# Recurrent-memory attention with a GeGLU block: TensorE work of the recurrent stage moved to column groups of 32, and one output written before another

## The chip, the cores and the metric

The kernel runs on one core of a Trainium2 chip. The metric is the device time of one execution in microseconds. The engines are TensorE (PE; its weight loads are listed as PEld), VectorE (DVE), ScalarE (ACT), GpSimd (POOL) and SyncE (SP). The kernel uses POOL and SP mostly to issue DMAs.

## The reference

All inputs are bf16. Two branches share the input `x` (2048 rows of 1024), and a gate for each row mixes them.

```python
def _A_ref(x, mem0, Wq, Wk, Wv, Wo, seg_len):       # 32 heads of 128, M = 8, seg_len = 32
    mask = (idx[:, None] < M) | (idx[:, None] >= idx[None, :])
    mem = mem0
    for s in range(n_seg):                          # 64 segments
        xs = x[:, s * seg_len:(s + 1) * seg_len, :]
        h = jnp.concatenate([mem, xs], axis=1)      # 40 rows
        q, k, v = (einsum('btd,dhe->bhte', h, W) for W in (Wq, Wk, Wv))
        scores = einsum('bhqe,bhke->bhqk', q, k) * scale
        p = softmax(where(mask, scores, -1e9))
        o = einsum('bhte,hed->btd', einsum('bhqk,bhke->bhqe', p, v), Wo)
        mem = o[:, :M, :]
        outs.append(o[:, M:, :])
    return concatenate(outs)

def _B_ref(x, w_gate, w_up, w_down):                # inner size 3584
    return gelu(x @ w_gate) * (x @ w_up) @ w_down

g = sigmoid((x * gate_w).sum(-1, keepdims=True))
out = g * _A_ref(...) + (1 - g) * _B_ref(...)
```

The eight memory rows that a segment gives are the first rows of the next one, so the 64 segments run one after the other.

## The kernel before

**Stages.** The first 600 us or so compute the GeGLU branch with matmuls that use all 128 columns of the array (lines 449 and 494) and transposes of `x` (line 336). Then come the 64 segments, which are called the recurrent stage here.

**A segment's rows.** The 40 rows are split: 24 rows of the segment and the 8 memory rows make `hT` (32 columns), and the 8 first rows of the segment ("ext" rows) do not depend on the memory, so they are computed for four segments at once (`xe`, 32 columns), one or two of the six projections in a segment, ahead of time. Their results go through DRAM (`qk_scr`, `v_scr`) and come back through `qkst` and `vt`.

**Weight streams.** With only 32 rows in a segment, the rows are the stationary operand, and the weights move past them. The four matmuls of one step use the same 32 stationary columns on the four column groups of the array, each with another 512 weight columns, and write 32 partitions each. They are called P (line 955: the projections q, k, v in two halves of 16 heads, eight steps each), E (line 849: the same for the ext rows), O (line 1109: the output projection, 32 steps of 256 columns) and OE (line 1090: the output projection of four segments' ext rows). Part of the weights stays in SBUF and PSUM; the rest is streamed anew in each segment from DRAM into `ring` (line 615, issued on SP). The ring has ten slots, a transfer fills two of them, and each is issued when PE is through with its slots.

**Attention.** Between the streams stand short blocks:
- T (line 993): four 128 x 128 transposes of the projection in `rows`, after which DVE or ACT copies them to `qk`. The ext rows have the same at line 880.
- S (line 1027): eight matmuls of 40 stationary and 40 moving columns, in pairs, one at output partition 0 and one at 64. DVE and ACT then do the softmax (lines 1034 to 1047) and write `pn`.
- P^T (line 1057): four transposes of `pn`, each of 80 stationary columns. DVE copies them to `ptb` (line 1062).
- P V (line 1068): four matmuls with 128 stationary columns of `vt` and 80 moving ones. ACT copies the result to `oT` and `oe`.

Each occurs four times in a segment (heads by eight). At the segment's end ACT copies the first memory result to `rows` (line 1338), two transposes (line 1354) turn it, and DVE writes it into `hT`.

**Output.** DVE multiplies by the gate and adds the other branch's rows: `bo` (line 1364), which four DMAs write out (line 1371). In every fourth segment (`s % 4 == 3`, the "o" segments) the ext rows of four segments are finished as well: DVE writes them into the first 256 columns of `pn` (line 1375), and four more DMAs write those out (line 1382). Both sets are issued on POOL, in the last segment on SP and ACT. `pn` is the buffer that the softmax of the next segment writes.

**Order.** The order of work on each engine is written out by hand, and a small scheduler (`_Sched`) turns reads and writes into semaphore waits. A DMA that reads a buffer holds back the buffer's next writer.

Of the kernel before, what the change touches and what calls it, by code (L numbers as in the profile page):

```python
# [128 lines left out]
def bass_gated_mix__memory_aug_recurrent_mem_tr__geglu_ffn__prompt_kernel(  # L129
# [21 lines left out]
    SEG = 32  # L151
# [16 lines left out]
    with ExitStack() as es:  # L168
# [639 lines left out]
        for s in range(NSEG):  # L808
# [52 lines left out]
            def end_ext(m, h, j):  # L861
                if s == 0:
                    rx, kx, sx = stage(m, h)
                else:
                    flush()
                    rx, kx, sx = rowsx[:, :], RX, "rowsx"
                op("act", lambda e: e.activation(rx, PB[B_X][:, :], ACTF.Copy), r=[P(B_X)], w=kx)  # L867
                if m == "v":
                    def put():
                        op("pool", lambda e: e.dma_start(v_scr[j, h, :, :, :, :].rearrange("g u r c -> (g u r) c"), rx),  # L870
                           r=kx, w=[("vscr", j, h)], dsem="%sv" % sx)
                    vput.append(put) if s == 0 else put()
                    return
                mi = "qk".index(m)

                def go(bank=B_T):
                    def mk(e):
                        ins = None
                        for i in range(4):
                            ins = e.transpose(PBV[bank][:, i * 128:(i + 1) * 128], rx[:, i * 128:(i + 1) * 128], ident[:, :])  # L880
                        return ins
                    op("pe", mk, r=[*kx, ("ident",)], w=[P(bank)])
                    return bank

                def put(bank):
                    st = rx.rearrange("p (u g r i) -> p u g r i", u=GR, g=4, r=EXT)
                    src = PBV[bank][:, 0:512].rearrange("p (i g u r) -> p u g r i", i=4, g=4, u=GR)

                    def cp(e):
                        ins = None  # L890
                        for u in range(GR):
                            ins = e.tensor_copy(st[:, u], src[:, u])  # L892
                        return ins
                    op("dve", cp, r=[P(bank)], w=kx)
                    op("pool", lambda e: e.dma_start(  # L895
                        qk_scr[j * GR:(j + 1) * GR, h, :, mi, :].rearrange("u p x -> p u x"),
                        rx.rearrange("p (u x) -> p u x", u=GR)),
                       r=kx, w=[("qkscr", j, h, mi)], dsem=sx)
                post.append((go, put))
# [89 lines left out]
            def emit_T(m, eng="dve"):  # L989
                def mk(e):  # L990
                    ins = None
                    for i in range(4):
                        ins = e.transpose(PBV[B_T][:, i * 128:(i + 1) * 128], rows[:, i * 128:(i + 1) * 128], ident[:, :])  # L993
                    return ins
                op("pe", mk, r=[("rows",), ("ident",)], w=[P(B_T)])
                src = PBV[B_T][:, 0:512].rearrange("p (i g c) -> p g c i", i=4, g=4)
                if eng == "act":
                    op("act", lambda e: e.activation(qk[:, m, :, 0:SEG, :], src, ACTF.Copy), r=[P(B_T)], w=[("qk", m)])
                else:
                    op("dve", lambda e: e.tensor_copy(qk[:, m, :, 0:SEG, :], src), r=[P(B_T)], w=[("qk", m)])  # L1000
# [19 lines left out]
            def emit_S(o, s=s):  # L1020
                def mk(e):
                    ins = None
                    for i in range(4):
                        for side in range(2):
                            p0 = SIDES[side]
                            gq = 2 * (o % 2) + side
                            ins = e.matmul(PB[B_S][p0:p0 + L, i * L:(i + 1) * L],
                                           lhsT=qk[:, 0, gq, :, i], rhs=qk[:, 1, gq, :, i], start=True, stop=True,
                                           skip_group_check=True)
                    return ins  # L1030
                op("pe", mk, r=[("qk", 0), ("qk", 1), ("qke",)], w=[P(B_S)])
                sv = PB[B_S][0:104, 0:4 * L].rearrange("p (i c) -> p i c", i=4)
# [20 lines left out]
            def emit_PT(o, s=s):  # L1053
                def mk(e):
                    ins = None
                    for i in range(4):
                        ins = e.transpose(PBV[B_PT][0:KEYS, i * 128:i * 128 + 104], pn[0:104, i, :], ident[0:104, 0:104])  # L1057
                    return ins
                op("pe", mk, r=[("pn", 0), ("pn", 2 * SEG), ("ident",)], w=[P(B_PT)])
                src = PBV[B_PT][0:KEYS, 0:512].rearrange("p (i two c) -> p i two c", i=4, two=2)[:, :, :, 0:L]  # L1060
                first = [("z", t) for t in range(NT)] + [("th", t) for t in range(NT)] if s == 0 and o == 0 else []
                op("dve", lambda e: e.tensor_copy(ptb[0:KEYS, :, :, :], src), r=[P(B_PT)], w=[("ptb",)] + first)  # L1062

            def emit_PV(o, s=s):
                def mk(e):
                    ins = None
                    for i in range(4):
                        ins = e.matmul(PB[B_PV][:, i * 80:(i + 1) * 80], lhsT=vt[0:KEYS, o % 2, i * 128:(i + 1) * 128],  # L1068
                                       rhs=ptb[0:KEYS, i, :, :].rearrange("p two c -> p (two c)"), start=True, stop=True)
                    return ins  # L1070
                op("pe", mk, r=[("vt", o % 2), ("vte", o % 2), ("vte", o % 2, 0), ("ptb",)], w=[P(B_PV)])
                src = PB[B_PV][:, 0:320].rearrange("p (i two c) -> p i two c", i=4, two=2)
                dst = oT[:, o % 2, :, :].rearrange("p (two i) c -> p i two c", two=2)
                u = s % GR
                dste = oe[:, o * 8:(o + 1) * 8, u * EXT:(u + 1) * EXT].rearrange("p (two i) c -> p i two c", two=2)
                op("act", lambda e: e.activation(dst, src[:, :, :, 0:SEG], ACTF.Copy), r=[P(B_PV)], w=[("oT", o % 2)])  # L1076
                op("act", lambda e: e.activation(dste, src[:, :, :, SEG:L], ACTF.Copy), r=[P(B_PV)], w=[("oe", o)])
                if o < 2 and s > 0:
                    load_vte(s, 1, o)
# [43 lines left out]
            def begin_o():  # L1123
# [4 lines left out]
                if "o" in jobs:  # L1128
                    for q in range(4):
                        op("pool", lambda e, q=q, j=jobs["o"]: e.dma_start(  # L1130
                            rowsx[32 * q:32 * q + 32, 0:256], b_scr[j * GR:(j + 1) * GR, q, NR:SEG, :]),
                           r=[("bscr", jobs["o"], y) for y in range(GR)], w=[("rowsx", q)], dsem="be%d" % q)

            if s == 0:
                emit_P("q", 0, (0,))
# [214 lines left out]
            if s + 1 < NSEG:  # L1350
                def mk_mem(e):
                    ins = None
                    for x in range(2):
                        ins = e.transpose(PBV[B_PT][:, x * 128:(x + 1) * 128], rows[:, x * 128:(x + 1) * 128], ident[:, :])
                    return ins
                op("pe", mk_mem, r=[("rows",), ("ident",)], w=[P(B_PT)])
                msrc = PBV[B_PT][:, 0:256].rearrange("p (c q r) -> p q c r", c=2, q=4)[:, :, :, NR:SEG]
# [3 lines left out]
                back(1)  # L1361
            if s == 0:
                flush()
            op("dve", lambda e, s=s, B_O=B_O: e.scalar_tensor_tensor(  # L1364
                out=bo[:, :], in0=PB[B_O][:, 0:256], scalar=gseg[:, s:s + 1], in1=bo[:, :], op0=ALU.mult, op1=ALU.add),
               r=[P(B_O)] + [("gseg", "%s%d" % (k, q)) for k in "ab" for q in range(4)], w=[("bo", x) for x in range(4)])
            for put, bank in ends:
                put(bank)
            last = s == NSEG - 1
            for x, (d, b) in enumerate(rows_of(s)):  # L1370
                op(("sp", "act")[x % 2] if last else "pool", lambda e, d=d, b=b: e.dma_start(d, b),  # L1371
                   r=[("bo", x)], w=[("out", s, x)], dsem="%s%d" % ("end" if last else "out", x))
            if "o" in jobs:
                j = jobs["o"]
                op("dve", lambda e, j=j: e.scalar_tensor_tensor(
                    out=pnz[:, 0:256], in0=PB[B_X][:, 0:256], scalar=ge[:, j:j + 1], in1=rowsx[:, 0:256],
                    op0=ALU.mult, op1=ALU.add),
                   r=[P(B_X)] + [("gseg", "e%d%d" % (q, u)) for q in range(4) for u in range(GR)] + RX,
                   w=[("pn", 0), ("pn", 2 * SEG)])
                for q in range(4):  # L1380
                    op(("sp", "act")[q % 2] if last else "pool",
                       lambda e, q=q, j=j: e.dma_start(first_rows(of, j, q), pnz[32 * q:32 * q + 32, 0:256]),
                       r=[("pn", 0)] + [("out", x, q) for x in range(max(0, j * GR - 1), j * GR + GR - 1)],
                       w=[("oute", j, q)], dsem="%s%d" % ("ende" if last else "oute", q))
            if s > GR and s % GR == 2 and s // GR + 2 < NG:
                load_xe(s // GR + 2)

# [40 lines left out]
```

## Time and profile before

| what | value |
|---|---|
| time, median of 3 runs | 2500.43 us (2494.03 to 2503.6) |
| profiled execution | 2493.11 us, its span in the profile 2491.2 us |
| mean granted TensorE clock | 0.993 |
| DMA packets | 293698, 780.59 MB, mean 313 GB/s |
| weight stream into `ring` | 1153 DMAs of 512 KB and 63 of 256 KB, median 6.2 and 5.9 us from issue to landing |
| T, line 993 | 1024 transposes, median 219 ns for one |
| S, line 1027 | 2048 matmuls, median 198 ns |
| P^T, line 1057 | 1024 transposes, median 209 ns |
| P V, line 1068 | 1024 matmuls, median 202 ns |

Matmuls are pipelined: the duration of one reaches from its start to its modelled end, and the next may start long before that. So what a matmul costs PE is read from start to start. The idle time in a timeline's brackets is that before an instruction on its engine, with what ended it. "issue" is time in which the engine waited for nothing that the profile shows.

### The profile page before, as it was taken

The numbers are of one execution on the slowest core, as the hardware profiler recorded it, in microseconds if no ns is written. First come the engines' busy times: TensorE is split into PE (matmuls) and PEld (weight loads), VectorE is DVE, ScalarE is ACT, GpSimd is POOL, SyncE is SP. The second block draws the span as 40 slices with busy tenths as digits, with TensorE's granted clock in tenths as the row PEclk, the third lists the DMA queues.
The fourth block names the chain that finished last, engine by engine and source line by source line (L and its number), as shares of the span: only waits on it lengthen the run. The fifth ranks groups of instructions, "written<-read, shape, count | busy, mean of one in ns | idle before, by whom it ended". The sixth has DMA issues, their size and how long they took to land.

```text
span 2491.2 us, 77615 instructions
## 1 busy us (share of the span) xinstructions
PE 2242.6 (90%) x33993; PEld 1110.2 (45%) x33993; DVE 1209.9 (49%) x3499; ACT 933.0 (37%) x2196; POOL 653.8 (26%) x1162
## 2 busy tenths in 40 slices
PE   9999999999889898888889888988898888888887
PEld 4444444444444444444444444444444444444443
DVE  5626264451445455445454545445454445454544
ACT  4314132220434344434344434434343444343433
POOL 1010103102332323232323323332323232323222
PEclk9999999999999999999999999999999999999999
DMA  8727354468999999999999999999999999999997
GB/s 270 260 71 255 97 179 123 144 231 287 320 335 368 351 363 366 358 348 360 351 365 360 365 345 365 359 359 353 346 362 349 366 349 359 345 371 359 365 367 291
DMA packets 293698, 780.59 MB, mean 313 GB/s; under 512 B 48840, under 2 KB 112568, under 8 KB 292592
## 3 DMA queue, kind: packets, MB, share of 16 engines
q1 hardware_dynamic: 249344, 720.25, 79.6%
q0 software_dynamic: 43872, 55.31, 7.1%
q8 instruction: 268, 4.39, 0.7%
q14 instruction: 70, 0.57, 0.1%
q10 hardware_dynamic: 144, 0.06, 0.0%
HBM read 748.00 MB, written 37.22 MB: 315 GB/s over the span
## 4 chain that ended last, share of the span: by engine, by line
PE 57%; DMA 26%; DVE 10%; issue 3%; ACT 2%; POOL 2%; DVEq 0%; POOLq 0%; ACTq 0%
DMA ring<-w_scr 21%; PE pbb L955 7%; PE pba L955 7%; PE pbc L849 4%; PE pbb L1109 3%; DMA out_dram<-pn 3%; PE pbe L1057 2%; PE pba L1109 2%; PE pba L449 2%; PE pbb L449 2%; PE pbc L449 2%; PE pbh L449 2%; PE pbe L449 2%; PE pbg L449 2%; PE pbf L449 2%
## 5 line engine op out<-in xcount | busy, mean ns | idle before, releaser
L955 PE MATMUL pba<-arena,hT 128*32 128x512 bf16 x4416 | 360.4, 383 | 0.4 <-issue 0.4
L955 PE MATMUL pbb<-arena,hT 128*32 128x512 bf16 x4416 | 354.7, 383 | 0.0
L721 POOL DMA_DIRECT2D vt<-v_scr x252 | 147.7, 588 | 429.3 <-PE pbe L1068 234.6
L1000 DVE COPY qk<-pbe 128x512 bf16<-128x512 bf16 x129 | 89.3, 692 | 260.0 <-PE pbe L993 253.7
L849 PE MATMUL pbc<-arena,xe 128*32 128x512 bf16 x2208 | 215.0, 383 | 0.7 <-ACT rowsx L867 0.5
L1040 ACT ACTIVATE pbd<-pbd 104x160 f32<-104x160 f32 x256 | 72.3, 283 | 381.6 <-DVE pbd L1038 381.6
L1062 DVE COPY ptb<-pbe 80x320 bf16<-80x320 bf16 x256 | 82.1, 321 | 273.5 <-PE pbe L1057 273.5
L1371 POOL DMA_DIRECT2D out_dram<-bo x252 | 125.9, 507 | 224.4 <-DVE bo L1364 222.5
L955 PE MATMUL pba<-ring,hT 128*32 128x512 bf16 x1478 | 152.5, 385 | 29.0 <-DMA ring<-w_scr 26.4
L955 PE MATMUL pbb<-ring,hT 128*32 128x512 bf16 x1474 | 150.8, 384 | 16.2 <-DMA ring<-w_scr 15.5
L961 ACT ACTIVATE rows<-pba 128x512 bf16<-128x512 f32 x128 | 76.6, 598 | 214.0 <-PE pba L955 213.9
L1047 DVE TENSOR_TENSOR pn<-pbd,rr 104x256 bf16<-104x256 f32 (+1 forms) x512 | 142.4, 319 | 28.3 <-DMA out_dram<-pn 20.0
L955 PEld LDWEIGHTS pba<-arena,hT 128*32 128x32 bf16 x4416 | 110.5, 96 | 92.6 <-issue 3.4
L955 PEld LDWEIGHTS pbb<-arena,hT 128*32 128x32 bf16 x4416 | 106.8, 96 | 90.7 <-issue 2.4
L895 POOL DMA_DIRECT2D qk_scr<-rowsx x60 | 47.5, 791 | 356.6 <-DVE rowsx L892 309.6
L961 ACT ACTIVATE rows<-pbb 128x512 bf16<-128x512 f32 x128 | 76.6, 598 | 169.5 <-PE pbb L955 169.1
L1057 PE MATMUL pbe<-ident,pn 104*80 104x104 bf16 x1024 | 95.6, 216 | 39.8 <-DVE pn L1047 29.6
L1109 PE MATMUL pba<-ring,oT 128*32 128x256 bf16 x1792 | 104.1, 279 | 25.9 <-DMA ring<-w_scr 18.7
L1041 DVE TENSOR_REDUCE rs<-pbd 104x4 f32<-104x160 f32 x256 | 83.2, 325 | 89.4 <-ACT pbd L1040 89.4
L1109 PE MATMUL pbb<-ring,oT 128*32 128x256 bf16 x1792 | 113.6, 277 | 13.8 <-DMA ring<-w_scr 9.1
L1076 ACT ACTIVATE oT<-pbe 128x256 bf16<-128x256 f32 x256 | 97.2, 380 | 76.4 <-PE pbe L1068 76.4
L1109 PE MATMUL pba<-arena,oT 128*32 128x256 bf16 x2176 | 112.4, 279 | 11.6 <-ACT oT L1076 10.6
(266 smaller groups left out, 4454.3 us busy)
## 6 DMA issues: line engine op xcount, KB each, us to landing
ring<-w_scr SPq DMA_DIRECT2D x1153, 512.0 KB, 6.2
arena<-in_B_w_gate_dram SPq DMA_DIRECT2D x27, 1024.0 KB, 5.4
arena<-in_B_w_up_dram SPq DMA_DIRECT2D x27, 1024.0 KB, 7.9
ring<-w_scr SPq DMA_DIRECT2D x63, 256.0 KB, 5.9
qkst<-qk_scr POOLq DMA_DIRECT2D x126, 64.0 KB, 5.4
qk_scr<-rowsx POOLq DMA_DIRECT2D x60, 128.0 KB, 5.1
arena<-in_B_w_down_dram SPq DMA_DIRECT2D x7, 1024.0 KB, 11.7
arena<-in_A_Wk_dram SPq DMA_DIRECT2D x6, 1024.0 KB, 6.6
```

The source lines that it names most:

```text
L449: ins = e.matmul(PB[bank][:, :], lhsT=wv[:, kc, col:col + 128], rhs=xb[:, kc, :], start=(kc == 0), stop=(kc == KC - 1))
L721: op("pool", lambda e: e.dma_start(vt[2 * SEG:KEYS, par, :], v_scr[s // GR, h, 2 * par:2 * par + 2, s % GR, :, :]), r=[("vscr", s // GR, h ...
L849: ins = e.matmul(PB[B_X][32 * gq:32 * gq + 32, :], lhsT=xe[:, us[-1], :], rhs=us[gq // 2][0][gq % 2], start=(n == 0), stop=(n == KC - 1), ...
L955: ins = e.matmul(PB[bank][32 * gq:32 * gq + 32, :], lhsT=hT[:, kc, :], rhs=us[gq // 2][0][gq % 2], start=(x == 0), stop=(x == KC - 1), ski ...
L961: op("act", lambda e: e.activation(rows[:, :], PB[bank][:, :], ACTF.Copy), r=[P(bank)], w=[("rows",)])
L1000: op("dve", lambda e: e.tensor_copy(qk[:, m, :, 0:SEG, :], src), r=[P(B_T)], w=[("qk", m)])
L1041: op("dve", lambda e: e.tensor_reduce(rsv, sv, AX.X, ALU.add), r=[P(B_S)], w=[("rs",)])
L1047: op("dve", lambda e, c0=c0, k0=k0, n=n: e.tensor_tensor(out=pn[0:104, :, c0:c0 + 2 * n].rearrange("p i (two c) -> p i two c", two=2), in0 ...
L1057: ins = e.transpose(PBV[B_PT][0:KEYS, i * 128:i * 128 + 104], pn[0:104, i, :], ident[0:104, 0:104])
L1076: op("act", lambda e: e.activation(dst, src[:, :, :, 0:SEG], ACTF.Copy), r=[P(B_PV)], w=[("oT", o % 2)])
L1109: ins = e.matmul(PB[B_O][32 * q:32 * q + 32, 0:256], lhsT=oT[:, o % 2, k, :], rhs=u[q // 2][:, (q % 2) * 256:(q % 2 + 1) * 256], start=(o ...
L1371: op(("sp", "act")[x % 2] if last else "pool", lambda e, d=d, b=b: e.dma_start(d, b), r=[("bo", x)], w=[("out", s, x)], dsem="%s%d" % ("en ...
```

## The change

Every transpose and matmul of the recurrent stage that used 128, 80 or 40 stationary columns is split so that each part uses at most 32 columns, and writes the partitions of one column group, as the weight streams do: T and the transposes of lines 880 and 1354 become four for one, S two for one (32 and 8 of its 40 columns), P^T three for one (32, 32 and 16), P V four for one. The results and their places are the same.

In the "o" segments the ext rows are now finished and sent out before the segment's own rows, by the new `out_first`: DVE's line 1375 goes ahead of line 1364, and the four DMAs of line 1382 ahead of the four of line 1371. In the last segment the order stays as it was.

```diff
@@ transposes of the ext rows (line 880)
-  ins = e.transpose(PBV[bank][:, i * 128:(i + 1) * 128], rx[:, i * 128:(i + 1) * 128], ident[:, :])
+  for y in range(0, 128, 32):
+      ins = e.transpose(PBV[bank][y:y + 32, i * 128:(i + 1) * 128],
+                        rx[:, i * 128 + y:i * 128 + y + 32], ident[:, :])
@@ emit_T (line 993), and likewise the memory's transposes (line 1354)
-  ins = e.transpose(PBV[B_T][:, i * 128:(i + 1) * 128], rows[:, i * 128:(i + 1) * 128], ident[:, :])
+  for j in range(0, 128, 32):
+      ins = e.transpose(PBV[B_T][j:j + 32, i * 128:(i + 1) * 128],
+                        rows[:, i * 128 + j:i * 128 + j + 32], ident[:, :])
@@ emit_S (line 1027)
-  ins = e.matmul(PB[B_S][p0:p0 + L, i * L:(i + 1) * L],
-                 lhsT=qk[:, 0, gq, :, i], rhs=qk[:, 1, gq, :, i], start=True, stop=True, ...
+  for c0, c1 in ((0, SEG), (SEG, L)):
+      ins = e.matmul(PB[B_S][SIDES[side] + c0:SIDES[side] + c1, i * L:(i + 1) * L],
+                     lhsT=qk[:, 0, gq, c0:c1, i], rhs=qk[:, 1, gq, :, i], start=True, stop=True, ...
@@ emit_PT (line 1057)
-  ins = e.transpose(PBV[B_PT][0:KEYS, i * 128:i * 128 + 104], pn[0:104, i, :], ident[0:104, 0:104])
+  for j in range(0, KEYS, 32):
+      n = min(32, KEYS - j)
+      ins = e.transpose(PBV[B_PT][j:j + n, i * 128:i * 128 + 104], pn[0:104, i, j:j + n], ident[0:104, 0:104])
@@ emit_PV (line 1068)
-  ins = e.matmul(PB[B_PV][:, i * 80:(i + 1) * 80], lhsT=vt[0:KEYS, o % 2, i * 128:(i + 1) * 128],
-                 rhs=ptb[0:KEYS, i, :, :].rearrange("p two c -> p (two c)"), start=True, stop=True)
+  for j in range(0, 128, 32):
+      ins = e.matmul(PB[B_PV][j:j + 32, i * 80:(i + 1) * 80],
+                     lhsT=vt[0:KEYS, o % 2, i * 128 + j:i * 128 + j + 32],
+                     rhs=ptb[0:KEYS, i, :, :].rearrange("p two c -> p (two c)"), start=True, stop=True,
+                     skip_group_check=True)
@@ end of a segment (from line 1361 on)
+  last = s == NSEG - 1
+  if not last:
+      out_first()              # lines 1375 and 1382
   op("dve", ... out=bo ...)    # line 1364
   for put, bank in ends:
       put(bank)
-  last = s == NSEG - 1
   for x, (d, b) in enumerate(rows_of(s)):
       op(... dma_start(d, b) ...)   # line 1371
-  if "o" in jobs:
-      ...                      # lines 1375 and 1382
+  if last:
+      out_first()
```

## The prediction

> **What bounds the kernel now.** I read the page first: engine shares and the chain that ended last.
>
> ```profile
> span 2491.2 us, 77615 instructions
> PE 2242.6 (90%) x33993; PEld 1110.2 (45%) x33993; DVE 1209.9 (49%) x3499; ACT 933.0 (37%) x2196; POOL 653.8 (26%) x1162
> PE 57%; DMA 26%; DVE 10%; issue 3%; ACT 2%; POOL 2%; DVEq 0%; POOLq 0%; ACTq 0%
> ```
>
> PE looks like the bound, but the chain gives a quarter to DMA, nearly all of it the weight stream into `ring`. So next came the windows: the recurrent stage (from the ACT copy of line 1338 at the end of segment 0, for 61 segments) and two neighbouring segments.
>
> ```profile
> 646.50:2425.50 1779.00, 1560.16 (x29562) 791.63 (x29562) 885.00 (x2939) 725.23 (x1738) 543.32 (x956) 1.00 0.98 357
> 1553.40:1583.20 29.80, 26.51 (x513) 13.36 (x501) 13.86 (x47) 12.14 (x30) 9.45 (x17) 1.00 0.96 342
> 1583.20:1610.90 27.70, 25.19 (x474) 12.77 (x474) 15.31 (x51) 12.12 (x29) 8.74 (x15) 1.00 1.01 378
> ```
>
> The last three columns are clock, DMA share and GB/s. A segment takes 1779/61 = 29.16 us and moves 29.16 x 357 = 10.4 MB, with DMA busy 98% of the time. The granted clock is full, so the clock plays no part. The second row follows an "o" segment: DMA 0.96 busy, 342 GB/s. The third is DMA at its best. So PE and DMA are nearly balanced, and only a little of any PE time saved can reach the end.
>
> The PE timeline around a 128-wide transpose in the recurrent stage, and around one in the GeGLU stage, shows what the change is about.
>
> ```profile
> 1500.64 0.39 PE L955 MATMUL pbb<-arena,hT 128*32 128x512 bf16 x4
> 1500.96 0.40 PE L993 MATMUL pbe<-ident,rows 128*128 128x128 bf16 x4
> 1501.29 0.40 PE L849 MATMUL pbc<-arena,xe 128*32 128x512 bf16 x4
> 1501.52 0.39 PE L955 MATMUL pbb<-ring,hT 128*32 128x512 bf16 x4
> ...
> 55.83 0.59 PE L449 MATMUL pbb<-arena 128*128 128x512 bf16 x2
> 56.26 0.61 PE L336 MATMUL pbe<-ident,arena 128*128 128x128 bf16 x8
> 56.70 0.59 PE L449 MATMUL pbc<-arena 128*128 128x512 bf16 x2
> ```
>
> Among 128-wide matmuls the transposes cost nothing extra: 0.44 us for eight, 56 ns each, and the stream keeps its step of 216 ns. Among 32-wide ones the first transpose starts 322 ns after the group before it, not 216, and the next group 327 ns after that, though four transposes at 56 ns are 224. So passing between widths costs about 105 ns each way; transposing itself does not.
>
> **The change, part by part: PE.** Steps from start to start are medians of the trace's records.
> - T (line 993, 256 blocks) and the transposes of line 880 (64): entry 322 - 216 = 106, exit 327 - 224 = 103. 320 x 0.209 = 67 us.
> - S (1027): entry 104 in the 94 blocks that do not follow P^T; 270 now against four sets at the 36 to 40 ns between its present pairs, 150: 120. 94 x 0.104 + 256 x 0.120 = 40 us.
> - P^T (1057): exit 308 - 4 x 46 = 124 in 192 blocks; entry about 110, of which I count half since P^T mostly waits for `pn` anyway (103 us over 229 waits): 24 + 14 = 38 us.
> - P V (1068): now 3 x 35 + 129 = 234, then 4 x 36 = 144, so 90 in 256 blocks; entry 106 in the 192 that do not follow P^T: 23 + 20 = 43 us.
> - Line 1354, half a T: exit 103, 63 times: 6 us; its entry lies under ACT's copy.
>
> Together 194 us, 3.1 us a segment. This takes a set of four 32-wide matmuls to cost what one 128-wide costs. The nearest rows are P's and O's streams: their four start within 10 ns, loads 3 to 4 ns apart, and the group takes 216 ns for 512 columns, 109 for 256. No row shows a set shorter than 109 ns. If that were a floor, T would take 4 x 109 = 436 ns, which is 106 + 327 again, and nothing is saved. I take the low value, since the pairs of S already start 36 ns apart after the 4 ns within a pair. That is the bound from both sides: 0 to 194 us.
>
> The Trainium skill's page TensorEngine Tiling (Array Packing), "Key Properties", has the same reason for the change: switching the tiling mode drains TensorE; the 105 ns agree. Its section "Instruction Overhead" speaks against it: some 60 cycles for each matmul, an estimate of 25 ns at 2.4 GHz, so 16 matmuls 400 ns and almost no gain. The 4 ns steps above disagree.
>
> Of the 3.1 us a part goes back into waits: between an S and its P^T stands a DVE and ACT chain of about 3 us that does not shorten, and P^T already waits for it in most cases. I take a quarter as lost. PE then needs 29.16 - 2.3 = 26.9 us a segment, of which 1.2 is waiting for the ring (75 us in all): 25.7 without DMA.
>
> **The first rows.** After an "o" segment `pn` holds output rows until their DMAs have read it, and the next softmax waits.
>
> ```profile
> 1555.68 2.01 POOL L1371 DMA_DIRECT2D out_dram<-bo  x4 [8.00 <-DVE bo L1364]
> 1557.68 2.37 POOL L1382 DMA_DIRECT2D out_dram<-pn  x4
> 1564.28 0.17 DVE L1043 TENSOR_TENSOR rr<-mx,bm 104x8 f32<-104x8 f32 x1
> 1566.55 0.56 DVE L1047 TENSOR_TENSOR pn<-pbd,rr 104x256 bf16<-104x256 f32 x2 [2.10 <-DMA out_dram<-pn]
> ```
>
> Moved first, the four `pn` issues go 2.0 us earlier on POOL, and DVE's step 0.4 us earlier. That covers this wait of 2.10; over the stage it is 20.0 us in 13 places. What moves behind: the four `bo` issues, 2.4 us later, whose buffer is next needed by `load_b` (line 735) some 10 us on; `bo`'s DVE step 0.4 us, and behind it DVE's copy to `vt` (line 944). All eight issues stay ahead of the `vt` loads (line 721), which do not move. The new rows' wait is for output rows of earlier segments, landed long before. If `load_b`'s cover were gone it would cost at most the 2.4 us in one segment of four. I count 15 us saved where DMA has idle time (0.96), none elsewhere.
>
> **Two floors that do not move.** DMA: 10.4 MB at the best row's 378 GB/s are 27.5 us; at today's rate with no idle time, 0.98 x 29.16 = 28.6.
>
> Instruction fetch: the change adds 3072 + 2048 + 2048 + 3072 + 768 + 378 = 11,386 matmuls and as many loads. PE has some 980 instructions a segment now; it will have about 1340.
>
> ```profile
> q8 instruction: 268, 4.39, 0.7%
> 1789.14 0.40 PE L1090 MATMUL pbc<-arena,oe 128*32 128x256 bf16 x6 [1.96 <-issue]
> ```
>
> 268 packets of 16 KB for 68,700 PE instructions: 256 each. The seven PE stalls of 1.57 to 1.96 us that are put down to "issue" all sit at instruction 193 to 196 of such a block, and each ends about 1.4 us after a packet's end. In the recurrent stage the next packet starts 2.5 us (0 to 4.7) after PE crosses a boundary, takes 1.06, and no boundary is passed sooner than 1.25 after it: 4.8 us a block on average, up to 7.0. The start grows with the ring transfers in flight: 1.5 us with two, 3.0 with five. Now 980 / 256 = 3.8 blocks, one in 7.6 us; afterwards 5.2, one in 5.5 at today's pace. 5.2 x 4.8 = 25.1 us, but the blocks are uneven (a block of O's stream lasts 32 x 0.109 = 3.5 us, one of P's 32 x 0.216 = 6.9), for which I add half a microsecond each: 5.2 x 5.3, about 28. The page Runtime: NRT & Kernel Launch of the Trainium skill, "Instruction fetch mechanics", has the block of 16 KiB and calls its cost mostly hidden; the 1.96 us disagree, and by the page this floor would be left out.
>
> **Sum.** PE 25.7, fetch about 28, DMA 27.5 to 28.6. They share one ring and do not overlap perfectly, so I take the upper end, 28.6: (29.16 - 28.6) x 62 = 35 us, the first rows' 15 within it. Profiled execution: 2493.1 us (span 2491.2 and 1.9 around it); 2493 - 35 = 2458. The median of the runs shown, 2500.4, lies 7 us above, so 2465.
>
> **Rivals.**
> - Fetch becomes the bound, slower. Place: each 256-instruction border of the recurrent stage. PE's faster blocks keep the ring's queue fuller, a turnaround rises to 3.0 + 1.06 + 1.3 = 5.4 us, and with uneven blocks 5.8: 5.2 x 5.8 = 30.2 us, 62 more us: 2562. It decides when turnaround and unevenness pass 29.16 / 5.2 = 5.6 us. For it: today's stalls. Against: a stalled PE frees no ring slots, and the fetch gets quicker (1.2 to 1.8 us to start after most stalls). Milder, it ends near 2530. Chance 0.27.
> - The sets do not run together (the floor of 109 ns), so only the first rows count, some of it lost to fetch: 2490 to 2505. For it: no row shows a shorter set; against: the steps of 4 ns. Chance 0.13. The Trainium skill's "Instruction Overhead" in TensorEngine Tiling (Array Packing) would lead here.
> - DMA reaches 378 GB/s throughout, being fed without a break: 27.6 us, 97 us less: 2403. For it: the third row; against: that segment begins with a filled ring. Chance 0.10.
> - The forecast: 0.50.
>
> About 0.5%, 12 us, is what a measurement can tell from no change. Faster takes the forecast's most part and the last rival, 0.58; same 0.14; slower 0.28. The range goes from the third rival's 2403 up to between the two figures of the first.
>
> **What would show it.** In the profile after: step into T 216, not 322, and T's 16 matmuls about 224 ns; DMA share of the recurrent stage 0.99 to 1.00; more ring waits on PE; no `out_dram<-pn` wait on DVE; some 357 instruction packets. The forecast is wrong if PE's "issue" waits grow from tens to hundreds of us, or if T still takes 430 ns from group to group.

## The result: 4% slower, and the profile after

The changed kernel takes 2598.56 us (median of 4 runs, 2596.33 to 2605.85), the kernel before 2502.01 on the same chip (2494.03 to 2509.39): ratio 1.0401, interval 1.0375 to 1.0427. The forecast was 2465 us. The loss is all in the recurrent stage: from the end of segment 0 to the end of segment 62 it lasts 1911.6 us instead of 1808.4, 30.83 us a segment instead of 29.17.

The page of the changed kernel: span, engines, chain by engine, and the instruction queue.

```profile
span 2596.6 us, 100387 instructions
PE 2164.6 (83%) x45379; PEld 1164.3 (45%) x45379; DVE 1205.4 (46%) x3499; ACT 937.7 (36%) x2196; POOL 652.1 (25%) x1162
PE 53%; DMA 26%; DVE 9%; issue 8%; ACT 3%; POOL 0%; SPq 0%; DVEq 0%; POOLq 0%; ACTq 0%
q8 instruction: 357, 5.85, 0.9%
```

PE is busy 78 us less, and the time is longer. On the chain "issue" went from 3% to 8%: time in which an engine, here mostly PE, waited for nothing that the profile shows and still did nothing. The recurrent stage in windows, 61 segments as before (the last three columns are clock, DMA share, GB/s):

```profile
645.50:2527.50 1882.00, 1489.87 (x40408) 845.33 (x40408) 880.90 (x2939) 730.66 (x1737) 542.02 (x956) 0.96 0.95 338
```

DMA fell from 0.98 busy to 0.95, so it is less of a bound than before; and the granted clock fell from 1.00 to 0.96. The PE timeline shows what the split did and what it cost: first a T that runs through, then a stretch at half clock, then a T that is cut in two.

```profile
721.74 0.50 PE L849 MATMUL pbc<-ring,xe 128*32 128x512 bf16 x4
721.95 0.39 PE L996 MATMUL pbe<-ident,rows 128*32 128x128 bf16 x10
722.17 0.38 PE L957 MATMUL pbb<-arena,hT 128*32 128x512 bf16 x1
722.17 0.28 PE L996 MATMUL pbe<-ident,rows 128*32 128x128 bf16 x6
...
728.35 0.68 PE L957 MATMUL pba<-arena,hT 128*32 128x512 bf16 x4
728.78 0.68 PE L996 MATMUL pbe<-ident,rows 128*32 128x128 bf16 x16
729.20 0.68 PE L957 MATMUL pba<-ring,hT 128*32 128x512 bf16 x4
729.63 0.68 PE L957 MATMUL pba<-arena,hT 128*32 128x512 bf16 x4
...
1896.81 0.33 PE L996 MATMUL pbe<-ident,rows 128*32 128x128 bf16 x9
1898.48 0.29 PE L996 MATMUL pbe<-ident,rows 128*32 128x128 bf16 x7 [1.34 <-issue]
```

The first T enters 216 ns after the group before it and takes 0.22 us: both width changes are gone. In the second stretch every step takes twice as long, 0.43 us from group to group. In the last T nine of the sixteen transposes run, then PE stands still for 1.34 us, with nothing but "issue" named: the instructions behind the border of a block of 256 had not arrived. The trace's instruction packet before it lasts from 1896.12 to 1897.05 us, and PE goes on 1.4 us after its end. Such stops have one place: with the PE records of the trace numbered in blocks of 256, 130 of the stage's gaps of over 0.5 us from start to start stand before number 193, and no other number has more than 6.

Counted over the stage from the trace's records (a stall is a gap of over 0.5 us at a border of 256 instructions; half clock is time in which the clock's records say 0.5; the last column is the mean time from a border to the start of the next instruction packet):

| kernel | instructions a segment | us a segment | stalls, us (number) | half clock, us | ring waits of PE, us | packet starts after, us |
|---|---|---|---|---|---|---|
| before | 977 | 29.17 | 31 (31) | 23 | 67 | 2.53 |
| after | 1332 | 30.83 | 200 (139) | 157 | 104 | 2.77 |

The stalls grew by 169 us. The streaming that fell into half-clock time cost some 60 us more than before, an estimate: half of the time in which columns streamed at that clock. The ring waits grew by 37. The sum, some 265 us, less the 103 us of the result leaves some 160 us that was gained elsewhere. This is a remainder, and not a measurement of what the split saved on PE.

### The profile page after: what moved, and what is told of

Read it like the earlier page. It is cut to its first block, busy times and chain, and to the rows that moved or that the text cites. A ratio compares the mean times of both kernels' runs of the same rounds, so it can differ in the third digit from the quotient of the medians.

```text
span 2596.6 us, 100387 instructions
## 1 busy us (share of the span) xinstructions
PE 2164.6 (83%) x45379; PEld 1164.3 (45%) x45379; DVE 1205.4 (46%) x3499; ACT 937.7 (36%) x2196; POOL 652.1 (25%) x1162
## 4 chain that ended last, share of the span: by engine, by line
PE 53%; DMA 26%; DVE 9%; issue 8%; ACT 3%; POOL 0%; SPq 0%; DVEq 0%; POOLq 0%; ACTq 0%
DMA ring<-w_scr 23%; PE pba L957 7%; PE pbb L957 6%; PE pbc L849 4%; PE pbb L1119 4%; PE pba L1119 3%; PE pbe L1063 2%; PE pbc L1100 2%; PE pbf L449 2%; PE pbg L449 2%; PE pbh L449 2%; PE pbe L449 2%; PE pbe L1076 2%; PE pba L449 2%; PE pbd L449 1%
## 5 line engine op out<-in xcount | busy, mean ns | idle before, releaser
L957 PE MATMUL pba<-arena,hT 128*32 128x512 bf16 x4416 | 372.1, 382 | 4.6 <-issue 4.5
L957 PE MATMUL pbb<-arena,hT 128*32 128x512 bf16 x4416 | 370.2, 385 | 6.7 <-issue 6.7
L849 PE MATMUL pbc<-arena,xe 128*32 128x512 bf16 x2208 | 234.6, 394 | 10.4 <-issue 9.5
L957 PEld LDWEIGHTS pba<-arena,hT 128*32 128x32 bf16 x4416 | 123.5, 99 | 84.4 <-issue 9.1
L1076 PE MATMUL pbe<-ptb,vt 80*32 80x80 bf16 x4096 | 96.2, 208 | 77.1 <-DVE ptb L1069 30.9
L957 PEld LDWEIGHTS pbb<-arena,hT 128*32 128x32 bf16 x4416 | 123.0, 99 | 83.5 <-issue 15.7
L1119 PE MATMUL pbb<-ring,oT 128*32 128x256 bf16 x1792 | 132.7, 293 | 31.1 <-issue 16.6
L1119 PE MATMUL pba<-arena,oT 128*32 128x256 bf16 x2176 | 128.9, 300 | 23.7 <-issue 13.0
L1119 PE MATMUL pba<-ring,oT 128*32 128x256 bf16 x1792 | 120.3, 299 | 32.9 <-DMA ring<-w_scr 20.7
L1119 PE MATMUL pbb<-arena,oT 128*32 128x256 bf16 x2176 | 123.7, 293 | 18.1 <-issue 11.9
```

The lines of the kernel that those rows point to most:

```text
L849: ins = e.matmul(PB[B_X][32 * gq:32 * gq + 32, :], lhsT=xe[:, us[-1], :], rhs=us[gq // 2][0][gq % 2], start=(n == 0), stop=(n == KC - 1), ...
L957: ins = e.matmul(PB[bank][32 * gq:32 * gq + 32, :], lhsT=hT[:, kc, :], rhs=us[gq // 2][0][gq % 2], start=(x == 0), stop=(x == KC - 1), ski ...
L1076: ins = e.matmul(PB[B_PV][j:j + 32, i * 80:(i + 1) * 80], lhsT=vt[0:KEYS, o % 2, i * 128 + j:i * 128 + j + 32], rhs=ptb[0:KEYS, i, :, :].r ...
L1119: ins = e.matmul(PB[B_O][32 * q:32 * q + 32, 0:256], lhsT=oT[:, o % 2, k, :], rhs=u[q // 2][:, (q % 2) * 256:(q % 2 + 1) * 256], start=(o ...
```

## The experiments

**The first rows alone.** No block split:

```diff
 kernel before
+ out_first() ahead of line 1364 and the DMAs of line 1371 (in the last segment: behind them, as before)
```

> The kernel before with the second part of the change alone: first rows finished and sent before the segment's own rows, no block split. Theory (instruction fetch is what costs; the new order is sound): 10 to 20 us faster than before, about 2485 us, and the DVE wait for out_dram<-pn (20 us) gone. Rival (the new order costs, by sending the segment's own rows later): slower than before by 20 us or more, and most of the 98 us of the whole change is found here.

2499.74 us, ratio 1.0002 (0.9984 to 1.0019): no change. The DVE row of the softmax's last step, first in the kernel before and then in this run, shows that the wait aimed at did go:

```profile
L1047 DVE TENSOR_TENSOR pn<-pbd,rr 104x256 bf16<-104x256 f32 (+1 forms) x512 | 142.4, 319 | 28.3 <-DMA out_dram<-pn 20.0
L1047 DVE TENSOR_TENSOR pn<-pbd,rr 104x256 bf16<-104x256 f32 (+1 forms) x512 | 142.4, 319 | 8.8
```

PE's own wait for `pn` fell by 11 us, but the segments after "o" segments last 30.11 us instead of 30.05. PE's ring waits are 6 us more. The half-clock time is 59 us instead of 23, but that says little: the profiled run of the kernel before had a granted clock of 0.993, its 43 runs on record 0.989 on average (0.982 to 0.994), and the ten runs of this one 0.988. Both theories missed, and what took the gain stays open.

**The split alone.**

```diff
 changed kernel
- out_first() ahead of line 1364
+ out_first() behind the DMAs of line 1371, as before
```

> The change without its second part: all blocks split into column groups of 32, the old order of the output rows. Theory (fetch): 2605 to 2620 us, that is the changed kernel's time plus what the first rows save, with some 190 us of PE stalls at the borders of 256 instructions. Rival (the order of the rows is at fault): about 2470 us.

2608.00 us, ratio 1.0427 (1.0376 to 1.0478), as expected, with 200 us of stalls and 185 us at half clock. So the split makes the whole loss. Against the whole change the intervals overlap: what the first rows are worth with it is not settled.

**More instructions without any split.** The kernel before, each P matmul in two halves of 256 columns:

```diff
-for gq in range(4):
-    ins = e.matmul(PB[bank][32 * gq:32 * gq + 32, :], lhsT=hT[:, kc, :],
-                   rhs=us[gq // 2][0][gq % 2], ...
+for hf in range(2):
+    for gq in range(4):
+        ins = e.matmul(PB[bank][32 * gq:32 * gq + 32, hf * 256:hf * 256 + 256], lhsT=hT[:, kc, :],
+                       rhs=us[gq // 2][0][gq % 2][:, hf * 256:hf * 256 + 256], ...
```

> The kernel before, no block split and the old order, but each P matmul of 512 columns written as two of 256: 12,288 more matmuls and as many loads, about what the change adds (11,386), in a place where the width of the column groups does not change. By start-to-start times 2 x 109 = 218 ns instead of 216, so 48 x 64 x 2 ns = 6 to 9 us of PE work. Theory (fetch): 1370 instructions a segment, 5.3 blocks of 256 at about 5.9 us, 31 us a segment or more and no width changes saved: 2620 to 2680 us, with stalls of 150 us or more at the borders of blocks. Rival (the 32-wide blocks themselves are slow, the number of instructions doesn't matter): 2505 to 2515 us.

2624.04 us, ratio 1.0511 (1.0470 to 1.0552). The queue on its page:

```profile
q8 instruction: 364, 5.96, 0.9%
```

And its recurrent stage in windows:

```profile
643.50:2552.40 1908.90, 1609.60 (x41274) 1130.34 (x41274) 885.16 (x2939) 723.65 (x1737) 543.26 (x956) 0.98 0.94 333
```

183 us of stalls at 134 borders, against 31 us in the kernel before, with the same T, S, P^T and P V, the same widths, and the 6 to 9 us of added PE work that was estimated (the halves step at 109 ns). The number of instructions alone brings the stalls. Ring waits fell to 19 us: PE is now nearly always the later of the two.

**S and P^T only.** Two of the splits, with the first rows first:

```diff
 changed kernel
- T, line 880, line 1354 and P V in column groups of 32
+ T, line 880, line 1354 and P V as before
```

> The change with only S and P^T split (4096 more matmuls, not 11,386), and the first rows first. Theory (fetch): 1110 instructions a segment, 4.3 blocks, one in 6.7 us at today's pace, so stalls at the borders stay below 70 us in all, while the widths saved around S and P^T (about 80 us of PE time) partly come through: 2465 to 2490 us, faster than before. Rival (each split block costs, whatever the fetch): a third of the change's loss, about 2520 us with the first rows' gain.

2519.73 us, ratio 1.0068 (1.0045 to 1.0091), slower where I expected faster, and just the rival's 2520. The stalls are as expected, 61 us, 30 more than before. What I had not reckoned with stands in two other places. PE's ring waits rose from 67 to 111 us, so that about half of the 80 us reckoned as saved on PE was handed to DMA. And the granted clock fell: 0.980 on average over its five runs, against 0.989. That each split block costs, whatever the fetch, is not ruled out by this run; the runs with half of the columns below speak against it.

**Half of the streamed bytes, by partitions.** Both kernels with ring transfers of partitions 0 to 63 alone:

```diff
-op("sp", lambda e: e.dma_start(ring[:, sl:sl + wd, :].rearrange(...), src), ...
+np_ = 128 if s == 0 else 64
+op("sp", lambda e: e.dma_start(ring[0:np_, sl:sl + wd, :].rearrange(...), src[0:np_]), ...
```

> The kernel before, with the ring's transfers after segment 0 loading only partitions 0 to 63 of each weight tile (half of the streamed bytes is left out). DMA then has about 5.7 MB a segment instead of 10.4 and is no bound. Theory (PE with its width changes is the bound right behind DMA): the 67 us of ring waits and part of the 31 us of fetch stalls go, some 2400 to 2425 us. Rival (fetch or PE hardly depend on the DMA load): 2430 us or more.

> The changed kernel with the same half of the streamed bytes left out. Theory (the next 256 instructions come late because their packet stands behind the ring's transfers): the packet starts about 1 us after a border instead of 2.8, the stalls fall from 200 us to under 60, and the split's PE gain of 2 to 3 us a segment shows: 2250 to 2330 us, 100 us or more below the kernel before with the same bytes left out. Rival (the fetch is slow by itself, whatever the DMA load): stalls stay above 120 us, and the time is no more than 40 us below it, or above it.

2436.32 us for the kernel before, 2497.16 for the changed one. These are the rivals' times, but the profile shows that the premise failed: with half the bytes DMA is still busy 0.88 of the stage in the one and 0.87 in the other. The packets start 1.58 and 2.07 us after a border, and the changed kernel still stalls 165 us.

**Half of the streamed bytes, by columns.** All partitions, but one slot of two, so packets of 2048 bytes:

```diff
-op("sp", lambda e: e.dma_start(ring[:, sl:sl + wd, :].rearrange(...), src), ...
+nw = wd if s == 0 else 1
+op("sp", lambda e: e.dma_start(ring[:, sl:sl + nw, :].rearrange(...), src[:, 0:nw * 1024]), ...
```

> The kernel before, with each of the ring's transfers after segment 0 loading only the first of its two slots: half of the streamed bytes is left out, on all partitions, in packets of 2048 bytes instead of 4096. DMA should be busy some 0.55 of the stage (halving the partitions left it at 0.87 and so did not unload it). Theory: PE-bound, the ring waits gone, 2420 to 2440 us as with half the partitions.

> The changed kernel with the same half of the streamed bytes left out (first slot of each transfer only). Theory (the instruction packet is late because it stands behind ring packets): with DMA at 0.55 it starts at most 1.5 us after a border instead of 2.8, stalls fall from 200 us to under 90, the split's gain shows, and the time is 20 to 110 us below the kernel before with the same bytes left out. Rival (the turnaround is PE's own, whatever DMA does): the packet still starts 2 us or more after a border, stalls stay above 140 us, and the time is above the kernel before with the same bytes left out.

2401.19 us (2401.15 to 2401.35, below the 2420 to 2440 expected) and 2373.00 (2369.39 to 2380.99): here the split is 28 us faster. The stage's windows of the kernel before with half the columns:

```profile
646.10:2337.10 1691.00, 1529.65 (x29562) 803.19 (x29562) 883.44 (x2939) 721.08 (x1738) 541.40 (x956) 1.00 0.67 205
```

And of the changed kernel with half the columns:

```profile
645.30:2304.70 1659.40, 1410.45 (x40408) 806.89 (x40408) 876.69 (x2939) 724.61 (x1737) 541.89 (x956) 0.99 0.69 210
```

DMA is 0.67 and 0.69 busy (0.55 was expected). The instruction packet starts 1.00 and 1.61 us after a border (1.5 at most was expected of the changed kernel), and the stalls are 8 and 52 us. The same 1332 instructions a segment that cost 200 us of stalls beside a full DMA cost 52 beside one that is 0.69 busy. So the loss needs both: more instructions, and a DMA that is late with them. The gain of 28 us also shows how little of the 194 us forecast on PE can come through even so: PE waits longer for `oT` (52 us against 40), for `qk` (29 against 8) and for the ext rows (27 against 7).

**Fewer ring transfers in flight.** First the ring's first transfers were issued later, by two slots and by four:

```diff
-slot_free(RING)
+slot_free(RING - 2)      # and RING - 4
```

> The changed kernel with at most four ring transfers in flight instead of five (two ring slots stay unused ahead of time), all work done. Theory (fetch waits behind the ring's transfers): the packet starts about 0.4 us sooner, stalls fall from 200 us to some 140, and the time by 20 to 60 us: 2540 to 2580. Rival (the packet's delay does not come from the ring's queue): stalls as before, the shallower prefetch adds ring waits, 2600 us or more.

> The changed kernel with at most three ring transfers in flight, all work done. Theory: the packet starts about 1 us sooner and the stalls fall below 120 us; whether the time falls depends on the ring waits, which grow as only 1.5 MB are under way: 2530 to 2620 us. Rival (delay independent of the ring's queue): stalls stay near 200 us and ring waits come on top, 2630 us or more.

2603.42 and 2610.09 us, ratios 1.0405 (1.0361 to 1.0449) and 1.0439 (1.0367 to 1.0511). The times, and some 200 us of stalls, are those of the changed kernel, but neither run puts the theory to the test: at most borders four or five transfers are still in flight, since each waits for its own slots only. A ring of eight slots does hold the number to four:

```diff
-RING = 10
+RING = 8
```

> The changed kernel with a ring of eight slots instead of ten, which does hold the transfers in flight to four (issuing the first ones later did not: each transfer waits for its slots alone, so five were still in flight). Theory (fetch waits behind the ring's transfers): no border finds five in flight, the packet starts some 0.3 to 0.5 us sooner, stalls 140 to 170 us; ring waits grow with the shallower prefetch, 2580 to 2640 us. Rival (delay independent of the number in flight): start 2.8 us after the border and stalls 185 us or more.

2702.81 us, ratio 1.0812 (1.0748 to 1.0876), above the 2580 to 2640 expected. The packet starts 2.59 us after a border, 0.2 sooner, less than the 0.3 to 0.5 expected. The stalls fall to 110 us, but PE now waits 300 us for the ring and so needs its instructions more slowly; which of the two brought the stalls down is not separated. Holding the number in flight down does not pay here.

**The memory's transposes only.** The cheapest of the splits, on the chain from segment to segment:

```diff
 kernel before, first rows first
+ line 1354 in column groups of 32
```

> The kernel before with the first rows first and only the memory's two transposes at the segment's end (line 1354) split: 378 more matmuls in all, 12 instructions a segment, on the chain from one segment to the next. Theory (any PE time saved is worth at most what DMA's 2% of idle time allow, a few more instructions cost nothing yet): 0.1 us a segment saved, 2494 to 2500 us, same or faster by up to 0.3%. Rival (every split block loses, also this one): slower than before by 5 us or more.

2498.58 us, ratio 0.9977 (0.9948 to 1.0007): no change that can be told. No version tried beats the kernel before with all its work done.

## Why the prediction was wrong, by its steps

- The widths. Right: the step into T is 216 ns, and from a block's first start to the next group's T takes 224 ns (327 before), S 151 (270) and P V 140 (234). A set of four 32-wide matmuls costs what one costs, and the floor of 109 ns is not there: T's sets step every 56 ns, P V's every 35. By the Trainium skill's page TensorEngine Tiling (Array Packing), "Instruction Overhead", a set of four would take about 100 ns, an estimate from its 60 cycles a matmul at 2.4 GHz; the trace's 56 and 35 ns disagree. The remainder of some 160 us found above does not contradict the 194, but it does not measure them either.
- The waits. I took a quarter of that as given back. With DMA out of the way the split and its 44 us of added stalls together gained 30 us of the stage, so only some 75 us came through: well over half is given back.
- The first rows. The wait went as forecast, the 15 us did not come: alone, the new order changed nothing (0.9984 to 1.0019).
- DMA's floor of 28.6 us. Not reached: the segment takes 30.83 us. Nor is it fixed: DMA is busy 0.945 of that, 29.1 us for the same bytes.
- Fetch. This is the step that failed: the sum set this floor of 28 us beside PE's 25.7 and DMA's 28.6 and took the largest of the three averages, so that a late packet cost nothing. Measured, the stalls cost 200 us, 3.2 us a segment, on top of the time that PE needs. The averages alone would give no stall: without its stall, but with all other waits, a block takes PE 5.3 us, and the turnaround, from a border until the next one can be passed, is 2.77 + 1.06 + 1.25 = 5.1 us. But both spread, the first from 3.7 to 7.2 us and the second from 3.4 to 6.8 (5% to 95% of the blocks), and it is decided border by border. In the blocks that end in a stall PE needed 4.6 us and the turnaround was 5.9. Counted block by block, the time by which the turnaround exceeds PE's need is 0.54 us on average, of the measured 0.62 us of stall a block, and it follows the stalls from block to block (correlation 0.985). The trace before had the sign already: 7.5 us a block against a turnaround of 4.8, and still 31 us of stalls.
- Fetch and DMA. They were put side by side as if each stood for itself. With DMA 0.67 busy the packet comes 1.0 us after a border, with DMA 0.98 busy 2.5 us. In the other direction DMA fell from 0.98 busy to 0.95 in the changed kernel; that this is because a stalled PE frees its slots late fits, but no run shows it by itself.
- The clock. The text said that it plays no part. In the profiled run before it played next to none, with 1.00 in the stage; the change brought it down to 0.96.
- The first rival came nearest, with its place and sign right. Its mechanism was right in part: it expected the packet 3.0 us after a border, and it comes after 2.77, a rise of 0.24 us. The argument held against it was wrong: after a stall the packet still took 2.6 us to start (median), not 1.2 to 1.8. Its 2562 us were 37 too few; it had no term for the clock, which by the estimate above is worth more than that.

## What to carry to other kernels

Count instructions as a resource of their own. Where TensorE is fed by small matmuls beside a saturated DMA, find how long it takes for a block of 256 instructions, and how long it is from a border until the next one can be passed (about 5 us here), before splitting anything. Compare the two block by block and not by their averages: a block with many short instructions stalls, and a later block with few does not make up for it. Taking out a change of width (105 ns each way here) pays only where the added instructions do not stall and where the stream is not the bound already. Two floors that feed each other give a time above both.

## What the runs showed of the hardware that was not expected

**The clock halves after windows that are not idle.** The half-clock times come in steps of 3.41 us on a fixed grid. I counted for each window of that grid the share of time in which matmul columns stream, at the 2.4 columns a ns that the 216 ns for 512 give. In the changed kernel the windows before a half-clock one have 8 to 42% (median 32%); those not before one have 34% at least, with a median of 72%. In the kernel before the limit lies in the same place: 39 to 44% against a median of 73%. In the changed kernel the longest standstill within such a window was 0.7 to 3.0 us (median 1.5), and 31 of 37 windows held a stall at a border. So one stall of 1.5 us with the usual waits beside it can be enough to halve the clock for the next 3.41 us. The Trainium skill's page TensorE: Matmul & The Clock Gate, Part 1, has the halving and the window of about 3.4 us, but after an idle window; in these two kernels no such window was idle throughout.

How much of the loss is the clock's alone was not tried: no run changed it by itself. The repeats give an estimate. Call clock loss the span times what the granted clock is short of 1. Over the 43 runs of the kernel before, 2487 to 2521 us, a run is 1.0 us longer for each us of clock loss (correlation 0.86). On average this loss is 28 us there (0.989) and 90 us in the changed kernel (0.966): 62 us more, close to the estimate above. A stall lengthens a run and lowers its clock at once, so this does not prove the cause.

**Instruction packets queue with data.** One 16 KB packet for each 256 instructions starts 1.0 us after a border beside a DMA that is 0.67 busy, and 2.5 beside one at 0.98. With two ring transfers in flight at the border it is 1.6 us in the changed kernel, with five 3.4, though with the ring of eight, where five are ruled out, the mean is only 0.2 us less.

**Half the partitions is not half the DMA time.** Ring transfers on 64 partitions moved half the bytes and kept DMA 0.88 busy; about the same bytes on 128 partitions took 0.67. A packet of 4096 bytes took 304 ns (median) on 64 partitions, against 159 ns in the kernel before.
